# Attention with soft MoE slots: twelve more score tiles exponentiated on VectorE, in two alternating chains

## The chip, the cores and the metric

The kernel runs on one core of one Trainium2 chip, in one launch. A core has five engines with queues of their own: TensorE (PE in the profile: matmuls into PSUM), VectorE (DVE), ScalarE (ACT: activations), GpSimd (POOL) and SyncE (SP, which here issues DMAs). Each engine takes its instructions in order and waits on semaphores for the others. The metric is the device time of the launch in microseconds (us), lower is better.

## The reference

Capped softmax attention over 8 batches of 12 heads, 448 tokens and head size 64, followed by a soft mixture of experts over the 3584 tokens with 32 slots (8 experts of 4):

```python
scores = scale * np.matmul(q, k.transpose(0, 1, 3, 2))      # scale = 1/8
scores = cap * np.tanh(scores / cap)                        # cap = 30
attn = np.exp(scores - scores.max(-1, keepdims=True))
attn = attn / (attn.sum(-1, keepdims=True) + 1e-09)
x = np.matmul(attn, v)              # then (batch * seq, heads * head_dim): (3584, 768)
logits = x @ phi                    # (3584, 32)
d = softmax(logits, axis=0)         # over tokens: what goes into a slot
slot_input = d.T @ x                # 8 experts x 4 slots x 768
slot_out = relu(slot_input @ w1) @ w2
out = softmax(logits, axis=1) @ slot_out
```

## The kernel before

**Tiles and chunks.** Two heads are stacked on the 128 partitions. A *pair* has seven *score tiles*, each of 128 partitions (64 keys of each of two heads) by 448 queries; 48 pairs give 336 tiles. Six tiles make a *chunk* (the array `exs[j]`, five of them in rotation), and the loop at line 655 runs over 56 chunks. Seven chunks are one batch, so the order of the work repeats with a period of seven.

**What happens to a chunk.** TensorE makes its scores in two halves of three tiles (`qk_chunk`, line 316) into two PSUM buffers. ScalarE takes each half with one tanh of 128x1344 (`tanh_chunk`, line 325) into `exs[j]` as float16. The exponential is then made in place. ScalarE does it with one instruction for the chunk (`exp_chunk`, `exp_part`, line 329), but only for the tiles from `taken(j)` on. The first `taken(j)` tiles (none, one or two) are made on VectorE by `poly_exp`: a chain of eight instructions on 16-bit data, lines 369 to 377. Step 0 scales and shifts the float16 value into a fixed-point exponent `y`, step 1 masks out its fraction into `xf`, steps 2 to 5 evaluate a cubic of it in `xp`, step 6 adds that to `y`, and step 7 turns it into the bits of a bfloat16. Five of the steps are TENSOR_SCALAR (0, 1, 2, 4, 7), three are TENSOR_TENSOR (3, 5, 6). Each step needs the one before it. There is one `xf` and one `xp`, two tiles wide, so a chain has to be past step 6 before the next one writes them.

**After the chunk.** When the last tile of a pair lies in chunk j, TensorE multiplies the pair's exponentials with V in the iteration of chunk j + 2 (`pv_first`, `pv_tail`, `pv_rest`, line 395), and VectorE takes the reciprocal of the sums (`norm`, line 402) and multiplies (line 405). Beside that VectorE copies transposed q and k (line 278) and x (line 457) out of PSUM, and small sums (lines 500, 508, 518, 543). GpSimd casts V (line 286) and issues the DMAs of q, k and the weights (lines 117, 121, 186).

**The order is written out.** The scheduling is manual: an engine's queue is what the program issues, in that order. One iteration has the slots 0, m, e, a, b, r, c, d between its fixed steps, and `at(j, slot, f, ...)` puts a job into a slot. A slot's jobs marked "<" come first, the unmarked ones then, the ones marked ">" last. Slot "r" lies between the reciprocal and the multiplication of `norm` where the iteration has a pv. The tables `SHARE` (by j mod 7) and `EDGE` (for single chunks) say for each chunk how many tiles VectorE takes and in which chunk and slot each of the eight steps is issued:

```python
SHARE = {0: (2, ((0, "<b"), (0, ">d"), (1, ">a"), (1, ">a"), (1, ">b"), (1, ">d"), (1, ">d"), (2, ">a"))),
...
for j, (tiles, places) in shared.items():
    for n, (dj, slot) in enumerate(places):
        at(j + dj, slot, poly_exp, j, tiles, n)
```

In these tables one chain is mostly finished, up to its last steps, before the next begins. Chunks with j mod 7 in {0, 2, 4, 5} give two tiles to VectorE, 6 gives one, 1 and 3 give none: nine of the 42 tiles of a period, 67 tiles in the whole run, in 39 chunks (28 with two tiles, 11 with one).

After the loop comes a tail with the last pairs, the logits and the slots (to about 260 us), the two expert layers, and the output.

Of the kernel before, what the change touches and what calls it, by code (L numbers as in the profile page):

```python
# [12 lines left out]
U16 = mybir.dt.uint16  # L13
F16 = mybir.dt.float16
# [4 lines left out]
P = 128  # L19
# [3 lines left out]
S = 448  # L23
# [14 lines left out]
def kernel(  # L38
# [27 lines left out]
    NCH = NTILE // CH  # L66
# [66 lines left out]

    att = ExitStack()
    ld = att.enter_context(tc.tile_pool(name="ld", bufs=1))
    NP = 2
    homes = {}
    for nm in ("qk0", "ex1", "wk", "ldv", "ex2", "ex3", "vb0", "qk1", "ex4", "ex0", "vb1"):
        homes[nm] = att.enter_context(tc.tile_pool(name=nm, bufs=1))
# [1 line left out]
    vb = [homes["vb0"], homes["vb1"]]  # L141
    qk = [homes["qk0"], homes["qk1"]]
    ldv, wk = homes["ldv"], homes["wk"]
    xf = wk.tile([P, NP * S], U16, name="xf")
    xp = wk.tile([P, NP * S], F16, name="xp")
    xs = att.enter_context(tc.tile_pool(name="xs", bufs=4))
    attp = ExitStack()
    psS = attp.enter_context(tc.tile_pool(name="psS", bufs=2, space=PSUM))
    psV = attp.enter_context(tc.tile_pool(name="psV", bufs=1, space=PSUM))
# [181 lines left out]
    def exp_chunk(j):  # L331
# [1 line left out]

    SHARE = {0: (2, ((0, "<b"), (0, ">d"), (1, ">a"), (1, ">a"), (1, ">b"), (1, ">d"), (1, ">d"), (2, ">a"))),
             2: (2, ((0, ">b"), (0, "<c"), (1, ">a"), (1, "<b"), (1, "<b"), (2, "e"), (2, ">a"), (2, "<b"))),
             4: (2, ((0, ">a"), (0, ">b"), (0, "<c"), (0, ">d"), (0, ">d"), (1, ">a"), (1, "<b"), (1, ">c"))),
             5: (2, ((0, "<d"), (0, "<d"), (1, ">a"), (1, ">a"), (1, "<c"), (1, "<d"), (1, "<d"), (2, "e"))),
             6: (1, ((0, "e"), (0, ">d"), (0, ">d"), (1, ">a"), (1, ">a"), (1, ">c"), (1, "<d"), (2, "<b")))}  # L340
    EDGE = {3: (1, ((0, ">b"), (0, ">b"), (0, "<c"), (0, ">c"), (0, ">d"), (1, ">a"), (1, ">a"), (1, "<b"))),
            4: (2, ((0, "<b"), (0, ">c"), (0, ">d"), (1, "e"), (1, "<b"), (1, "<b"), (1, ">c"), (2, "r"))),
            48: (1, ((0, "e"), (0, ">d"), (0, ">d"), (1, ">a"), (1, ">a"), (1, "<c"), (1, "<d"), (2, "<b"))),
            49: (2, ((0, "<b"), (0, ">d"), (0, ">d"), (1, ">a"), (1, ">b"), (1, ">d"), (1, ">d"), (2, ">a"))),
            51: (2, ((0, "e"), (0, ">a"), (0, ">a"), (0, "<d"), (0, ">d"), (1, "e"), (1, ">b"), (1, ">c"))),
            52: (1, ((0, "<b"), (0, ">b"), (0, "<c"), (0, "<d"), (1, "e"), (1, "e"), (1, "<b"), (1, ">b"))),
            53: (1, ((0, "e"), (0, ">b"), (0, "<c"), (0, ">c"), (0, ">d"), (1, "<b"), (1, ">b"), (1, ">d"))),
            54: (1, ((0, "<d"), (0, "<d"), (0, "<d"), (1, "e"), (1, "<a"), (1, "<a"), (1, ">a"), (1, ">a")))}
    shared = {j: SHARE[j % 7] for j in range(3, NCH - 2)
              if j % 7 in SHARE and j + SHARE[j % 7][1][-1][0] < NCH - 1}  # L350
    shared.update(EDGE)

    octaves = cap * math.log2(math.e)
    base = math.ceil(octaves) + 1
    if base + octaves > 127:
        shared = {}

    def taken(j):
        return shared[j][0] if j in shared else 0
# [4 lines left out]
    def poly_exp(j, tiles, n):  # L364
        n1 = tiles * S
        t = exs[j][:, 0:tiles, :].rearrange("p u s -> p (u s)")
        y, f, p = t.bitcast(U16), xf[:, 0:n1], xp[:, 0:n1]
        steps = (
            lambda: dve.tensor_scalar(y, t.bitcast(F16), octaves * STEP, base * STEP + c0,  # L369
                                      ALU.mult, ALU.add),  # L370
            lambda: dve.tensor_scalar(f, y, STEP - 1, None, ALU.bitwise_and),  # L371
            lambda: dve.tensor_scalar(p, f, c3, c2, ALU.mult, ALU.add),  # L372
            lambda: dve.tensor_tensor(p, p, f, op=ALU.mult),  # L373
            lambda: dve.tensor_scalar(p, p, c1, None, ALU.add),  # L374
            lambda: dve.tensor_tensor(p, p, f, op=ALU.mult),  # L375
            lambda: dve.tensor_tensor(y, y, p, op=ALU.add),  # L376
            lambda: dve.tensor_scalar(y, y, 128.0 / STEP, 128.0 * (127 - base),
                                      ALU.mult, ALU.add))
        steps[n]()
# [173 lines left out]
    def at(j, slot, f, *a):  # L553
        if j < 0:
            j, slot = 0, "b"
        aux.setdefault((j, slot), []).append((f, a))
# [21 lines left out]
    for b in range(B):  # L578
        j, p = b * PER, 6 * b

        def when(nm):
            return j + WHEN[nm][0], WHEN[nm][1]
# [17 lines left out]
        if b < B - 1:  # L600
# [5 lines left out]
                at(*when("en"), e_norm, b)  # L606
            if b % 2:
                at(*when("es"), e_sums, b // 2)
    for j, (tiles, places) in shared.items():
        for n, (dj, slot) in enumerate(places):  # L610
            at(j + dj, slot, poly_exp, j, tiles, n)
    for n, job in enumerate(wjobs):
        at(1 + n * (NCH - 5) // len(wjobs), "b", *job)
    for j, slot, n in ((0, "a", 10), (0, "c", 10), (1, "b", 10), (1, "c", 8)):
# [207 lines left out]
    for n0, half in sorted(w2_spilled, key=lambda x: (x[1], x[0])):  # L822
        t = tl.tile([P, 4, HD], BF16, name=f"w2t{n0}_{half}")
# [123 lines left out]
    for n in range(B // 2 * NT):  # L947
        bb, c = divmod(n, NT)
# [15 lines left out]
        if n == NH or c == 0 or full:  # L964
            ob, n1 = wts.tile([P, 2, 2, HD], F32, name="ob", tag="w1", bufs=E), n
# [44 lines left out]
```

## Time and profile before

| | |
|---|---|
| median of 3 runs | 295.72 us (295.69 to 295.93) |
| span of the profiled execution, first to last instruction | 293.9 us |
| busy over the span: PE, DVE, ACT, POOL | 255.4, 240.4, 260.3, 138.2 us |
| VectorE, steps of `poly_exp`, 39 of each | lines 369 to 377 |
| ScalarE, tanh (line 325) | 113 instructions, 147.5 us |
| ScalarE, exponentials (line 329) | 58 instructions, 119.5 us |
| granted TensorE clock, mean over the span | 0.985 |

The span leaves out what lies around the first and the last instruction, 1.8 us against the median. In the page, the mean of an instruction is its own duration; two instructions of one engine can overlap, so a count times a mean can exceed the busy time. Where what one instruction really costs its engine is wanted, it is read from the distance between two starts. A line such as "L375 DVE TENSOR_TENSOR xp<-xp,xf" is an instruction of line 375 on VectorE that writes `xp` from `xp` and `xf`.

### The profile page before, as it was taken

How to read it: one execution, taken by the hardware profiler on the slowest of the kernel's cores; microseconds unless marked ns; L12 is line 12 of the kernel's file. 1: busy time of each engine (PE TensorE's matmuls, PEld its weight loads, DVE VectorE, ACT ScalarE, POOL GpSimd, SP SyncE). 2: the span in 40 equal slices, each digit the busy share in tenths (PEclk: the TensorE clock that was granted, in tenths of full speed). 3: DMA queues.
4: the chain of work that ended last, by engine and by line, in shares of the span. 5: the costliest groups of instructions: out<-in, count | busy, mean ns of one | idle time of the engine just before them, and what ended most of it. 6: DMA issues, size and time to landing. Idle time of an engine off the chain costs nothing.

```text
span 293.9 us, 10870 instructions
## 1 busy us (share of the span) xinstructions
PE 255.4 (87%) x4728; PEld 173.9 (59%) x4728; DVE 240.4 (82%) x554; ACT 260.3 (89%) x211; POOL 138.2 (47%) x200
## 2 busy tenths in 40 slices
PE   8898889998999899979988998899989899998620
PEld 6655556756675667556756675667566668542300
DVE  3728998999999999999999989999999976246740
ACT  4999999999999999999999999999999997237620
POOL 4593554763676367635673658365643220300000
PEclk9999999999999999999999999999999999999985
DMA  7999999999999999999999999999999567989896
GB/s 273 217 194 206 221 176 212 203 191 218 230 218 193 210 228 224 199 208 227 189 179 217 223 217 184 216 229 228 209 191 219 131 216 237 407 321 376 323 427 287
DMA packets 58561, 68.13 MB, mean 232 GB/s; under 512 B 4241, under 2 KB 54673, under 8 KB 58513
## 3 DMA queue, kind: packets, MB, share of 16 engines
q0 software_dynamic: 42448, 35.31, 77.8%
q1 hardware_dynamic: 15776, 31.89, 30.8%
q8 instruction: 37, 0.61, 0.8%
q10 hardware_dynamic: 288, 0.23, 0.2%
q14 instruction: 12, 0.09, 0.1%
HBM read 91.72 MB, written 19.27 MB: 378 GB/s over the span
## 4 chain that ended last, share of the span: by engine, by line
PE 35%; DVE 32%; ACT 21%; issue 4%; DMA 2%; POOL 2%; DVEq 0%; SPq 0%; ACTq 0%
PE pv L395 12%; ACT ex L325 11%; ACT ex L329 9%; PE sc L316 6%; DVE xq L405 4%; DVE ex L376 3%; DVE xp L375 3%; DVE xp L373 3%; DVE xf L371 2%; DVE xp L372 2%; DVE ex L369 2%; DVE kT L278 2%; DVE xp L374 2%; DVE qT L278 2%; PE so_ps L878 2%
## 5 line engine op out<-in xcount | busy, mean ns | idle before, releaser
L325 ACT ACTIVATE ex<-sc 128x1344 f16<-128x1344 f32 (+1 forms) x113 | 147.5, 1410 | 1.7 <-PE sc L316 1.6
L329 ACT ACTIVATE ex<-ex 128x1792 bf16<-128x1792 f16 (+5 forms) x58 | 119.5, 2064 | 0.1
L395 PE MATMUL pv<-vbd,ex 128*128 128x130 bf16 (+1 forms) x1610 | 94.4, 211 | 6.2 <-POOL vbd L286 2.7
L395 PEld LDWEIGHTS <-ex 128*128 128x128 bf16 (+1 forms) x1680 | 75.7, 101 | 34.1 <-PE sc L316 9.2
L316 PE MATMUL sc<-qT,kT 64*64 64x448 bf16 x672 | 70.5, 359 | 4.0 <-ACT ex L325 1.6
L286 POOL CAST vbd<-vraw 64x896 bf16<-64x896 f32 x46 | 44.1, 959 | 52.8 <-PE pv L395 37.3
L316 PEld LDWEIGHTS <-kT 64*64 64x64 bf16 x672 | 24.5, 105 | 10.0 <-issue 5.8
L405 DVE TENSOR_TENSOR xq<-pv,rec 128x448 bf16<-128x448 f32 x46 | 28.7, 624 | 1.6
L117 POOL DMA_DIRECT2D w1b<-in_moe_w_dram x32 | 24.9, 781 | 0.0
L488 POOL COPY e<-E 128x512 bf16<-128x512 bf16 x9 | 6.3, 705 | 37.4 <-PE eps L507 19.9
L376 DVE TENSOR_TENSOR ex<-ex,xp 128x896 uint16<-128x896 uint16 (+1 forms) x39 | 21.8, 559 | 1.2
L294 POOL MEMSET vbd<- 64x1 bf16 x22 | 3.0, 136 | 41.1 <-PE pv L395 41.1
L375 DVE TENSOR_TENSOR xp<-xp,xf 128x896 f16<-128x896 f16 (+1 forms) x39 | 22.0, 563 | 0.4
L373 DVE TENSOR_TENSOR xp<-xp,xf 128x896 f16<-128x896 f16 (+1 forms) x39 | 21.6, 554 | 0.7
L276 PE MATMUL qps<-ident,qb 128*64 128x128 bf16 x308 | 12.8, 221 | 8.5 <-DVE kT L278 6.6
L278 DVE COPY kT<-kps 128x896 bf16<-128x896 bf16 x23 | 14.3, 622 | 6.1 <-PE kps L276 5.7
L276 PEld LDWEIGHTS <-qb 128*64 128x64 bf16 x308 | 10.9, 109 | 13.7 <-issue 13.2
L425 PE MATMUL pv<-ones 128*128 128x57 bf16 x474 | 18.6, 188 | 0.0
L372 DVE TENSOR_SCALAR xp<-xf 128x896 f16<-128x896 uint16 (+1 forms) x39 | 17.8, 456 | 0.5
L186 POOL DMA_DIRECT2D qb<-in_q_dram x22 | 16.7, 759 | 3.0 <-DMA kraw<-in_k_dram 3.0
L371 DVE TENSOR_SCALAR xf<-ex 128x896 uint16<-128x896 uint16 (+1 forms) x39 | 17.3, 444 | 0.3
L457 DVE COPY xT<-xps 128x896 bf16<-128x896 bf16 (+1 forms) x24 | 14.4, 600 | 3.0 <-PE xps L448 2.5
(135 smaller groups left out, 365.5 us busy)
## 6 DMA issues: line engine op xcount, KB each, us to landing
w1b<-in_moe_w_dram POOLq DMA_DIRECT2D x32, 384.0 KB, 8.6
vraw<-in_v_dram SPq DMA_DIRECT2D x44, 224.0 KB, 6.1
w2d<-in_moe_w_dram POOLq DMA_DIRECT2D x21, 384.0 KB, 9.5
w2t<-w2d SPq DMA_DIRECT2D x21, 384.0 KB, 7.2
out_dram<-ob SPq DMA_DIRECT2D x7, 768.0 KB, 7.6
qb<-in_q_dram POOLq DMA_DIRECT2D x22, 224.0 KB, 7.3
kb<-in_k_dram POOLq DMA_DIRECT2D x22, 224.0 KB, 6.2
out_dram<-obh SPq DMA_DIRECT2D x23, 192.0 KB, 2.0
```

What stands on the lines that cost most here:

```text
L117: pool.dma_start(out=w1b[e][:, js, fs], in_=w1r[:, e, js, fs])
L276: pe.transpose(ps[h * HP:h * HP + HP, c, :], src[:, h, c * DH:(c + 1) * DH], ident)
L278: dve.tensor_copy(t, ps)
L286: pool.tensor_copy(vbds[Q % 2][r, :, :, c0:c0 + DH], raw[r])
L316: pe.matmul(sc[cs, u, 0:S], qkT["k", Q][r, c, cs], qkT["q", Q][r, :, cs], start=True, stop=True)
L325: act.activation(exs[j][:, half * CS + u0:half * CS + u1, :].bitcast(F16), sc[:, u0:u1, 0:S], ACT.Tanh, scale=qk_scale / cap)
L329: act.activation(exs[j][:, u0:u1, :], exs[j][:, u0:u1, :].bitcast(F16), ACT.Exp, scale=cap)
L373: lambda: dve.tensor_tensor(p, p, f, op=ALU.mult),
L375: lambda: dve.tensor_tensor(p, p, f, op=ALU.mult),
L376: lambda: dve.tensor_tensor(y, y, p, op=ALU.add),
L395: pe.matmul(out_, exs[j][r, u, q0:q0 + (HP if tail else P)], v_, start=(c == 0 and g == gs[0] < NF), stop=(c == NT - 1), skip_group_check= ...
L405: dve.tensor_tensor(xq[Q][:, h, s0:s1, :], pv[:, 0:s1 - s0, 0:DH], rec.to_broadcast([P, s1 - s0, DH]), op=ALU.mult)
```

## The change

A second, one tile wide pair of work buffers `xf[1]`, `xp[1]` is added, in a pool of its own behind the others. `SHARED` gives for each chunk the number of tiles on VectorE and which pair of buffers its chain uses; `POLY` gives for each chunk and slot the steps issued there, as (chunk of the chain, step). In `POLY` the steps of two chains, one on each pair of buffers or the end of one and the start of the next, mostly take turns. The period now has four chunks with two tiles and three with one, eleven of 42 tiles; in the run 79 tiles in 51 chunks (28 with two, 23 with one). The function's steps themselves are the same.

```diff
-    NP = 2
...
-    xf = wk.tile([P, NP * S], U16, name="xf")
-    xp = wk.tile([P, NP * S], F16, name="xp")
     xs = att.enter_context(tc.tile_pool(name="xs", bufs=4))
+    more = att.enter_context(tc.tile_pool(name="more", bufs=1))
+    room = tuple(enumerate(zip((wk, more), (2, 1))))
+    xf = [home.tile([P, n * S], U16, name=f"xf{x}") for x, (home, n) in room]
+    xp = [home.tile([P, n * S], F16, name=f"xp{x}") for x, (home, n) in room]
...
-    SHARE = {0: (2, ((0, "<b"), (0, ">d"), (1, ">a"), (1, ">a"), (1, ">b"), (1, ">d"), (1, ">d"), (2, ">a"))),
...
+    SHARED = {3: (2, 0), 4: (1, 0), 5: (1, 1), 6: (2, 0), 7: (2, 0), 8: (1, 1), 9: (2, 0), 10: (1, 1),
...
+              19: (1, 1), 20: (2, 0), 21: (2, 0), 22: (1, 1), 23: (2, 0), 24: (1, 1), 25: (2, 0), 26: (1, 1),
...
+    POLY = {(3, '>b'): ((3, 0),),
...
+            (22, '>a'): ((22, 0), (21, 3), (20, 7), (22, 1)),
+            (22, '>b'): ((21, 4), (22, 2)),
+            (22, '<c'): ((21, 5),),
+            (22, '>c'): ((21, 6),),
+            (22, '>d'): ((22, 3), (21, 7)),
+            (23, '>a'): ((23, 0), (22, 4)),
+            (23, 'r'): ((22, 5),),
+            (23, '<c'): ((23, 1),),
+            (23, '>d'): ((23, 2), (23, 3), (22, 6)),
+            (24, 'e'): ((24, 0),),
+            (24, '>a'): ((22, 7), (24, 1), (23, 4)),
+            (24, 'r'): ((24, 2),),
+            (24, '<c'): ((23, 5), (24, 3)),
+            (25, 'e'): ((23, 6), (25, 0), (23, 7)),
+            (25, '>a'): ((25, 1),),
+            (25, '>b'): ((24, 4),),
+            (25, 'r'): ((24, 5),),
+            (25, '<c'): ((25, 2),),
+            (25, '>c'): ((25, 3), (24, 6)),
...
-        y, f, p = t.bitcast(U16), xf[:, 0:n1], xp[:, 0:n1]
+        x = shared[j][1]
+        y, f, p = t.bitcast(U16), xf[x][:, 0:n1], xp[x][:, 0:n1]
...
-    for j, (tiles, places) in shared.items():
-        for n, (dj, slot) in enumerate(places):
-            at(j + dj, slot, poly_exp, j, tiles, n)
+    for (j, slot), ops in POLY.items():
+        for chunk, n in ops:
+            at(j, slot, poly_exp, chunk, shared[chunk][0], n)
```

## The prediction

> **What bounds the kernel now.** I read the page first (ScalarE, ACT, 89% busy; TensorE, PE, 87%; VectorE, DVE, 82%), then the stages. Nearly all idle time lies at the ends, so the share over the span misleads: the attention loop has to be read by itself.
>
> ```profile
> core 0: us, PE busy (x) PEld busy (x) DVE busy (x) ACT busy (x) POOL busy (x), PEclk, DMA share, GB/s
> 30.00:240.00 210.00, 192.33 (x3843) 136.05 (x3844) 198.19 (x460) 209.56 (x156) 117.86 (x167) 1.00 1.16 206
> ```
>
> In the 210 us of the loop ScalarE is busy 209.56: it is the bound. VectorE is busy 198.19, 94%. Whether the other 6% is free decides this case, because the change takes work off ScalarE and puts it on VectorE. So next the waits of VectorE in this stretch, the whole answer:
>
> ```profile
> DVE rec L402 <- PE pv L395: 2.2, 9, 0.4
> DVE xT L457 <- PE xps L448: 1.7, 3, 0.7
> DVE kT L278 <- PE kps L276: 1.4, 6, 0.6
> ```
>
> Only 5.3 us of real waiting. The rest of the 6% is small gaps, and they have a pattern, seen in VectorE's own timeline (start, duration, line):
>
> ```profile
> 130.24 0.38 DVE L375 TENSOR_TENSOR xp<-xp,xf 128x448 f16<-128x448 f16 x1
> 130.66 0.39 DVE L376 TENSOR_TENSOR ex<-ex,xp 128x448 uint16<-128x448 uint16 x1
> 130.97 0.39 DVE L371 TENSOR_SCALAR xf<-ex 128x896 uint16<-128x896 uint16 x1
> 131.39 0.59 DVE L372 TENSOR_SCALAR xp<-xf 128x896 f16<-128x896 uint16 x1
> 132.01 0.62 DVE L373 TENSOR_TENSOR xp<-xp,xf 128x896 f16<-128x896 f16 x1
> ```
>
> L376 uses what L375 has just written: it starts 0.42 us after it, 0.035 us behind its end. L371 belongs to another chain: it starts 0.31 us after L376, 0.08 us before that one ends. Over 30 to 240 us, taking starts and ends instruction by instruction: 264 starts lie on average 81 ns before the end of the one ahead, 164 lie 34 ns behind it, 31 come after a longer wait (6.3 us in all). A direct successor in the same chain thus costs about 117 ns more than a neighbour from elsewhere. That is the time the alternate placing can win.
>
> The fourth row shows the second loss: L372 took 0.59 us, where the same form takes 0.38 undisturbed. Beside it GpSimd (POOL) was issuing a DMA:
>
> ```profile
> 131.00 0.76 POOL L121 DMA_DIRECT2D w2d<-in_moe_w_dram  x1
> ```
>
> Of the 180 TENSOR_SCALAR steps of the chains in this stretch, 66 had no GpSimd instruction beside them and ran 4 ns over their undisturbed time on average; the other 114 ran 120 ns over, 14.0 us in all (86 ns for each two-tile step, 51 for each one-tile step). The TENSOR_TENSOR steps hardly moved (0.62 throughout).
>
> **The change, part by part.** One period is seven chunks. Before, it had four chunks with two tiles on VectorE and one with one; afterwards four with two and three with one. Over the run the two-tile chunks stay at 28 and the one-tile chunks go from 11 to 23: twelve more one-tile chains, and a new order.
>
> *ScalarE.* The price of a tile is read from starts, since its instructions overlap too:
>
> ```profile
> 122.76 1.91 ACT L329 ACTIVATE ex<-ex 128x1792 bf16<-128x1792 f16 x1
> 124.35 2.68 ACT L325 ACTIVATE ex<-sc 128x1344 f16<-128x1344 f32 x2
> 126.69 2.30 ACT L329 ACTIVATE ex<-ex 128x2240 bf16<-128x2240 f16 x1
> 128.65 2.78 ACT L325 ACTIVATE ex<-sc 128x1344 f16<-128x1344 f32 x2
> ```
>
> Four tiles hold ScalarE from 122.76 to 124.35, 1.59 us; five from 126.69 to 128.65, 1.96. A tile is 0.373 us (the finer stamps: 1.587 and 1.960), and twelve are 4.5 us. That is the whole possible gain.
>
> *VectorE.* The eight steps of a one-tile chain, from the groups by form over the whole run:
>
> ```profile
> L375 DVE TENSOR_TENSOR xp<-xp,xf 128x448 f16<-128x448 f16 x11 | 4.3, 391 | 0.1
> L376 DVE TENSOR_TENSOR ex<-ex,xp 128x448 uint16<-128x448 uint16 x11 | 4.3, 391 | 0.3
> L373 DVE TENSOR_TENSOR xp<-xp,xf 128x448 f16<-128x448 f16 x11 | 4.2, 381 | 0.0
> L369 DVE TENSOR_SCALAR ex<-ex 128x448 uint16<-128x448 f16 x11 | 3.9, 358 | 0.0
> L371 DVE TENSOR_SCALAR xf<-ex 128x448 uint16<-128x448 uint16 x11 | 3.7, 337 | 0.1
> L372 DVE TENSOR_SCALAR xp<-xf 128x448 f16<-128x448 uint16 x11 | 3.4, 312 | 0.3
> L374 DVE TENSOR_SCALAR xp<-xp 128x448 f16<-128x448 f16 x11 | 3.0, 275 | 0.3
> L377 DVE TENSOR_SCALAR ex<-ex 128x448 uint16<-128x448 uint16 x11 | 3.0, 270 | 0.0
> ```
>
> They sum to 2.715 us with collisions. The undisturbed times (the fastest tenth of each form, in step order 265, 266, 276, 380, 276, 383, 391, 268 ns) sum to 2.505. Twelve chains are 96 instructions:
> - Undisturbed: 12 x 2.505 = 30.1 us.
> - Every added instruction that starts 82 ns before its neighbour ends gives that back: 96 x 0.082 = 7.9.
> - Direct successors: I wrote out VectorE's queue from both tables and the loop's slots and counted pairs in which the second needs the first. There are 173 before (46 of them reciprocal then multiply) and 67 after (19, since a step is placed between them in slot "r"). 106 fewer x 0.117 = 12.4 us won.
> - So VectorE's queue grows by 30.1 - 7.9 - 12.4 = 9.8 us without collisions.
> - Collisions: 60 more TENSOR_SCALAR steps, at the one-tile mean of 51 ns, 3.0 us. Bounds: 0, if GpSimd, whose work does not change, only has so much to give; 5.2, at the two-tile mean of 86. I take 3.0, the row of the same form.
>
> [...]
>
> *Waits.* VectorE works on chunks 3 to 55 from 20.6 to 244.6 us, 224.0 us. In it, waits of over 45 ns add up to 8.0, so its queue alone needs 216.0, and afterwards 216.0 + 9.8 + 3.0 = 228.8. That is more than the 224.0 of now and than the 219.5 that ScalarE would need: VectorE becomes the bound. Which waits stay? The first (1.6 us for the first pv, chunk 3) and those of chunk 54 (0.9) stem from TensorE's order and stay. The waits in between are mostly for TensorE, itself paced by ScalarE; with VectorE late they mostly close. Those for a pv that needs a just finished chain stay: between the last step of a chain and the reciprocal behind it VectorE has 0.60 to 1.17 us of other steps in chunks 21 to 25, against 0.75 to 1.36 before. I keep 0.3 us per period, 1.8 in all. Together 4.3 us; bounds 0 and 8.0.
>
> *The rest.* Two buffers of 896 bytes in each partition, behind the others: nothing else moves. No DMA is added or moved; GpSimd, SP and TensorE keep their instructions, and where VectorE is late TensorE waits at pv, and behind it in its queue the scores of the next chunk, hence ScalarE. This is how the loss reaches the end; two score buffers and the one chunk between QK and pv let no more than a few us of lateness through unseen. TensorE was granted its full clock (1.00) at 92% busy; at 89% I cost that at nothing. If the clock did fall, the loop's TensorE work (192 us) has 18 us of room.
>
> **The sum.** 228.8 + 4.3 - 224.0 = +9.1 us. The profiled execution has a span of 293.9 us and would have 303.0. The median of the runs, 295.72, is 1.8 above the span; that lies around it and stays. 295.7 + 9.1 = 304.8 us. As a cross-check, one period: VectorE's queue without collisions goes from 26.3 to 27.9 us, ScalarE's from 29.5 to 28.8; with collisions (2.1, afterwards 2.5), 0.3 of small stretch elsewhere and 0.3 of waits VectorE needs 31.0, 1.5 more than the 29.5 of now; over six and a half periods that is 9.8.
>
> **The rivals.**
> - *ScalarE stays the bound and the gain arrives: 291.2* (295.7 - 4.5). VectorE would have to fit into 219.5. Even with no wait at all it has 225.8 without added collisions, so the 14 us of collisions would have to shrink by 6.3; to come out faster at all, by 1.8. For it: which step GpSimd meets is a matter of placing, and every step is placed anew. Against it: the load that GpSimd puts there is the same and VectorE spends more time in the steps that collide. 0.09. Landing within 0.2% (0.6 us, about what a measurement of this kernel can tell from no change): 0.03.
> - *Collisions do not grow, VectorE is the bound*: 216.0 + 9.8 + 2.5 - 224.0 = +4.3, 300.0. For it: GpSimd's work is fixed. 0.10.
> - *A convoy*: the waits do not close but grow, since a late chain makes pv late and pv the reciprocal: 8.0 kept and 0.5 us more per period, 228.8 + 8.0 + 3.2 - 224.0 = +16, 311.7. It decides when VectorE is later than TensorE at more than one reciprocal per period. Against it: the 0.94 at two of the four tight places is about the 0.9 us that a pv's last 15 matmuls took. 0.10.
> - *Alternating brings no overlap*, every added instruction at full length and no successor won: 12 x 2.715 = 32.6, so 216.0 + 32.6 + 4.3 - 224.0 = +28.9, 324.6. [...] The 264 early starts speak against it here. 0.02.
>
> **How the numbers follow.** The forecast of a VectorE bound with some more collisions has 0.66. Slower: 0.66 + 0.10 + 0.10 + 0.02 = 0.88; same 0.03; faster 0.09. The range takes in the bounds of collisions and waits: low +3.3 (the second rival, with the wait of chunk 54 gone too, rounded), 299.0; high 216.0 + 9.8 + 5.2 + 8.0 - 224.0 = +15.0, 310.5. Outside lie the faster and the equal cases, the missing overlap and part of the convoy.
>
> **What would show it.** Right: ScalarE below 97% busy in the loop, waiting for TensorE's scores, and those for VectorE at pv; VectorE with hardly a gap; direct successors down to about a third; one-tile TENSOR_SCALAR rows near or above their means of now; a chunk period of about 31 us. Wrong: ScalarE still at 99% and a period under 29.5 us, that is, VectorE's steps collide less; or waits of VectorE at the reciprocal of over 10 us in all, that is the convoy.

## The result, and the profile after

The changed kernel takes 314.4 us (median; 313.3 to 317.8) against 295.8 for the kernel before: a ratio of 1.064, 95% interval 1.057 to 1.070. It is slower by 18.5 us. Forecast were 9.1 us more, and at most 14.8: the direction was right, the size was not. The profiled execution has a span of 311.5 us.

The loop of the changed kernel, engine by engine (the window is longer because the loop is):

```profile
core 0: us, PE busy (x) PEld busy (x) DVE busy (x) ACT busy (x) POOL busy (x), PEclk, DMA share, GB/s
30.00:255.00 225.00, 193.40 (x3832) 133.96 (x3824) 219.64 (x557) 207.89 (x156) 119.71 (x165) 1.00 1.11 193
```

ScalarE, busy for 99.8% of the loop before, is at 92% (207.89 of 225). VectorE is at 97.6%; of the other 5.4 us 3.1 are waits and 2.2 the short gaps between neighbours. The waits say who holds whom, first ScalarE's, then VectorE's (the longest of the copies of x, 0.9, ends at 29.9 us, just ahead of the window), then the two of TensorE that are for VectorE's multiplication:

```profile
ACT ex L326 <- PE sc L317: 11.1, 18, 0.9
ACT E L718 <- PE lps L702: 5.8, 6, 1.2
```

```profile
DVE xT L693 <- PE xps L684: 2.4, 6, 0.9
DVE rec L638 <- PE pv L631: 0.9, 2, 0.7
DVE qT L279 <- PE qps L277: 0.5, 2, 0.3
DVE kT L279 <- PE kps L277: 0.2, 1, 0.2
```

```profile
PE pv L631 <- DVE xq L641: 12.9, 19, 1.1
PE junk L874 <- DVE xq L641: 6.7, 7, 1.0
```

(`junk` is a filler matmul whose result nobody uses; it takes the same PSUM buffer as a pv.) ScalarE, which had next to no waits, now waits 16.9 us for TensorE; TensorE waits 19.6 us for the multiplication, where in the whole run before its pv waited 1.1 us for it and the filler 1.6; VectorE waits 4.0 in all. VectorE is the bound, as forecast. But its queue is longer than the sum said, and one group shows where. VectorE's groups by form in this window, the two TENSOR_TENSOR steps of the cubic, one tile wide:

```profile
L611 DVE TENSOR_TENSOR xp<-xp,xf 128x448 f16<-128x448 f16 x22 | 16.2, 737 | 0.1
...
L609 DVE TENSOR_TENSOR xp<-xp,xf 128x448 f16<-128x448 f16 x22 | 10.4, 474 | 0.1
```

These two are the same operation on the same tiles, steps 5 and 3 of a chain. Before, they took 391 and 381 ns. Step 5 now takes 737 on average. Its place is what differs: the new table puts many of the fifth steps into slot "r", between the reciprocal and the multiplication. The timelines of VectorE and of GpSimd at one such place:

```profile
122.54 0.26 DVE L610 TENSOR_SCALAR xp<-xp 128x448 f16<-128x448 f16 x1
122.81 0.20 DVE L638 RECIPROCAL rec<-pv 128x7 f32<-128x7 f32 x1
122.93 1.05 DVE L611 TENSOR_TENSOR xp<-xp,xf 128x448 f16<-128x448 f16 x1
123.90 0.61 DVE L641 TENSOR_TENSOR xq<-pv,rec 128x448 bf16<-128x448 f32 x1
```

```profile
122.81 0.92 POOL L287 CAST vbd<-vraw 64x896 bf16<-64x896 f32 x1 [1.24 <-PE pv L631]
```

GpSimd's cast of V is released by the end of a pair's pv, because only then may the old V be overwritten. The reciprocal is released by the same event. Here they start together (122.81 both), and the cast takes 0.92 us. The step in slot "r" starts 0.12 us into it and runs 1.05 us instead of 0.38, to 0.25 us behind the end of the cast; the multiplication comes that much later. In the kernel before the same cast stood beside the reciprocal and the multiplication, which reads PSUM and was not held:

```profile
133.07 0.20 DVE L402 RECIPROCAL rec<-pv 128x7 f32<-128x7 f32 x1
133.31 0.62 DVE L405 TENSOR_TENSOR xq<-pv,rec 128x448 bf16<-128x448 f32 x1
133.85 0.61 DVE L457 COPY xT<-xps 128x896 bf16<-128x896 bf16 x1
```

```profile
133.22 0.95 POOL L286 CAST vbd<-vraw 64x896 bf16<-64x896 f32 x1
```

Here the 0.95 us of the cast lie beside 0.62 us of multiplication, and then beside a copy out of PSUM: neither is longer than elsewhere (0.62 and 0.61 us, and 0.62 is the mean of each in the loop). Counted over the whole run, 27 steps stand in slot "r" and overran their undisturbed times by 15.0 us. Of the 27, 25 lie beside a cast; the other two (at 23.2 and 156.3 us) overran by nothing. All other chain steps together overran by 9.1, less than the 15.7 of all steps before.

Beside the cast, the step with both inputs in SBUF took 1.05 us instead of 0.38, and the multiplication, one of whose inputs lies in PSUM, 0.62, its mean.

### The profile page after: what moved, and what is told of

It is laid out like the page before. It is cut to its first block, busy times and chain, and to the rows that moved or that the text cites. A ratio compares the mean times of both kernels' runs of the same rounds, so it can differ in the third digit from the quotient of the medians.

```text
span 311.5 us, 10979 instructions
## 1 busy us (share of the span) xinstructions
PE 258.0 (83%) x4728; PEld 173.7 (56%) x4728; DVE 262.3 (84%) x650; ACT 258.8 (83%) x211; POOL 140.2 (45%) x200
## 4 chain that ended last, share of the span: by engine, by line
DVE 65%; PE 20%; ACT 5%; issue 3%; DMA 2%; POOL 1%; DVEq 0%; ACTq 0%; SPq 0%
DVE xp L611 9%; DVE xq L641 8%; DVE ex L612 6%; DVE xp L609 6%; DVE ex L613 5%; PE pv L631 5%; DVE xf L607 4%; DVE xp L610 4%; DVE xp L608 4%; DVE ex L605 4%; DVE xT L693 4%; DVE qT L279 4%; DVE kT L279 3%; DVE rec L638 2%; ACT ex L326 2%
## 5 line engine op out<-in xcount | busy, mean ns | idle before, releaser
L326 ACT ACTIVATE ex<-sc 128x1344 f16<-128x1344 f32 (+1 forms) x113 | 142.5, 1292 | 12.6 <-PE sc L317 12.4
L631 PE MATMUL pv<-vbd,ex 128*128 128x130 bf16 (+1 forms) x1610 | 97.4, 213 | 23.2 <-DVE xq L641 13.7
L330 ACT ACTIVATE ex<-ex 128x1792 bf16<-128x1792 f16 (+5 forms) x58 | 108.2, 1870 | 0.1
L287 POOL CAST vbd<-vraw 64x896 bf16<-64x896 f32 x46 | 45.4, 988 | 56.1 <-PE pv L631 41.9
L611 DVE TENSOR_TENSOR xp<-xp,xf 128x896 f16<-128x896 f16 (+1 forms) x51 | 34.8, 682 | 0.5
L609 DVE TENSOR_TENSOR xp<-xp,xf 128x896 f16<-128x896 f16 (+1 forms) x51 | 28.0, 548 | 0.3
L612 DVE TENSOR_TENSOR ex<-ex,xp 128x896 uint16<-128x896 uint16 (+1 forms) x51 | 27.1, 531 | 0.1
L613 DVE TENSOR_SCALAR ex<-ex 128x896 uint16<-128x896 uint16 (+1 forms) x51 | 22.7, 446 | 0.1
L608 DVE TENSOR_SCALAR xp<-xf 128x896 f16<-128x896 uint16 (+1 forms) x51 | 20.3, 397 | 0.2
L607 DVE TENSOR_SCALAR xf<-ex 128x896 uint16<-128x896 uint16 (+1 forms) x51 | 18.5, 362 | 0.3
L661 PE MATMUL pv<-ones 128*128 128x57 bf16 x474 | 18.6, 188 | 0.0
L610 DVE TENSOR_SCALAR xp<-xp 128x896 f16<-128x896 f16 (+1 forms) x51 | 17.7, 347 | 0.2
## 6 DMA issues: line engine op xcount, KB each, us to landing
vraw<-in_v_dram SPq DMA_DIRECT2D x44, 224.0 KB, 5.6
qb<-in_q_dram POOLq DMA_DIRECT2D x22, 224.0 KB, 6.7
kb<-in_k_dram POOLq DMA_DIRECT2D x22, 224.0 KB, 5.6
```

The lines of the kernel that those rows point to most:

```text
L287: pool.tensor_copy(vbds[Q % 2][r, :, :, c0:c0 + DH], raw[r])
L326: act.activation(exs[j][:, half * CS + u0:half * CS + u1, :].bitcast(F16), sc[:, u0:u1, 0:S], ACT.Tanh, scale=qk_scale / cap)
L330: act.activation(exs[j][:, u0:u1, :], exs[j][:, u0:u1, :].bitcast(F16), ACT.Exp, scale=cap)
L631: pe.matmul(out_, exs[j][r, u, q0:q0 + (HP if tail else P)], v_, start=(c == 0 and g == gs[0] < NF), stop=(c == NT - 1), skip_group_check= ...
```

## The experiments

In what follows, "overrun" is the time of the chain steps above their undisturbed times, summed from VectorE's first chain step to the last multiplication of the loop.

**Slot r emptied.** The 27 steps go right behind the multiplication:

```diff
-            at(j, slot, poly_exp, chunk, shared[chunk][0], n)
+            at(j, "<c" if slot == "r" else slot, poly_exp, chunk, shared[chunk][0], n)
```

> The changed kernel, but every step that stood in slot r (between the reciprocal and the multiplication of a pair, 27 of them) is issued right behind the multiplication, first in slot c. Theory 1 (the steps in slot r run into GpSimd's cast of V, which starts when a pair's pv ends, and are held until it is done: 15.0 of the 24.1 us by which the chain steps overran): the cast (0.93 us) now runs beside the reciprocal and the multiplication (0.78 us together), so each step loses at most some 0.15 us: 15.0 - 4 gained, 27 x 0.117 = 3.2 lost since reciprocal and multiplication are direct neighbours again: about 8 us faster than the changed kernel, 306 (303 to 309). Theory 2 (collisions depend on how many steps there are, wherever they stand, and VectorE's longer queue is the cause): the step behind meets the same GpSimd instruction, and only the 3.2 us are lost: 315 to 318. Theory 3 (late chains make TensorE late and TensorE the reciprocal): within 2 us of the changed kernel, 312 to 316.

Measured: 300.2 us, ratio 1.015 (1.013 to 1.018) to the kernel before. That is 14 us faster than the change, more than any theory gave. The group of step 5, by form over 30 to 240 us:

```profile
L611 DVE TENSOR_TENSOR xp<-xp,xf 128x448 f16<-128x448 f16 x22 | 8.7, 395 | 0.1
```

It is back at 395 ns. The overrun fell from 24.1 to 11.9 us, VectorE's waits from 7.9 to 5.6. Theories 2 and 3 fall. The remaining 4.3 us over the kernel before are the part that the prediction had reasoned about: VectorE is still the bound.

**The same in the kernel before.** Four steps a period are moved from just ahead of the reciprocal into slot r:

```diff
-    SHARE = {0: (2, ((0, "<b"), (0, ">d"), (1, ">a"), (1, ">a"), (1, ">b"), ...
+    SHARE = {0: (2, ((0, "r"), (0, ">d"), (1, ">a"), (1, ">a"), (1, "r"), ...
-             2: (2, ((0, ">b"), ...
+             2: (2, ((0, "r"), ...
-             4: (2, ((0, ">a"), (0, ">b"), ...
+             4: (2, ((0, ">a"), (0, "r"), ...
```

> The kernel before, with four steps of each period moved into slot r, from just ahead of the reciprocal to between reciprocal and multiplication (chunks with j mod 7 in 0, 1, 2, 4; about 25 in the run). Same tiles, same buffers, same number of instructions. Theory 1: each moved step meets the cast and is held some 0.5 to 0.65 us, 12 to 16 us on VectorE, of which the 6 us of waits in the loop hide a part: 301 to 307. Theory 2: no step more, so no collision more, 25 x 0.117 = 2.9 us off VectorE's queue, and ScalarE remains the bound: 295 to 296.5.

Measured: 315.0 us, ratio 1.066 (1.062 to 1.070). With the tiles, buffers and instructions of the kernel before, this edit alone costs 19 us, as much as the whole change. One of the places, here with a TENSOR_SCALAR step:

```profile
126.05 0.21 DVE L402 RECIPROCAL rec<-pv 128x7 f32<-128x7 f32 x1 [0.23 <-PE pv L395]
126.17 1.05 DVE L371 TENSOR_SCALAR xf<-ex 128x896 uint16<-128x896 uint16 x1
127.15 0.61 DVE L405 TENSOR_TENSOR xq<-pv,rec 128x448 bf16<-128x448 f32 x1
```

What follows is from the profiled execution, the slowest of the five (319.1 us; VectorE's first chain step starts 2.9 us later in it than before). The 24 steps in slot r overran by 17.1 us. That is more than expected for each (0.71), and the waits did not hide any of it: they rose from 8.0 to 15.6. VectorE's waits over 30 to 255 us:

```profile
DVE rec L402 <- PE pv L395: 9.8, 31, 1.9
```

The late multiplication frees the PSUM buffer of pv late, so the next pv starts late (TensorE's pv waits 18.5 us for the multiplication, 1.1 before), and the next reciprocal waits for it. Here the convoy does exist.

**Without the casts.** The changed kernel and the kernel just described, with the casts left out from the third quad on (a quad, `Q`, is two pairs):

```diff
-        pool.tensor_copy(vbds[Q % 2][r, :, :, c0:c0 + DH], raw[r])
+        if Q < 2:
+            pool.tensor_copy(vbds[Q % 2][r, :, :, c0:c0 + DH], raw[r])
```

> The changed kernel without GpSimd's casts of V from the third quad of heads on (44 of 48 casts are left out, so V of these quads is missing from the result); all DMAs and all work of VectorE, ScalarE and TensorE stay. Theory 1: the chain steps lose the 19.4 us of overrun beside GpSimd's casts and copies but for some 3 us of the copies of e: 14 to 16 us faster than the changed kernel, 298 to 301, with the steps in slot r at their undisturbed times. If the issuing of DMAs on GpSimd were the main cause (4.7 us of overrun beside it): 311 to 315. Theory 3 (waits): no change, 312 to 316.

> e2_before_r (315.0) without GpSimd's casts of V from the third quad of heads on (V of these quads is missing from the result). Theory 1 (steps in slot r cost time only because of the cast beside them): the moved steps run at 0.38 and 0.27 us and the whole 19 us are gone, 293.5 to 296. If it were the late multiplication as such (TensorE waiting for the pv's buffer): 305 or more.

Measured: 295.3 us (ratio 0.998, 0.994 to 1.001) and 296.9 us (ratio 1.001, 0.997 to 1.005). The steps in slot r now overran by nothing (-0.8 and -0.9 us, that is, they ran at their undisturbed times), and 19 and 18 us are gone. The first ends 2.7 us below its range, the second 0.9 above. The casts are the cause, with slot r unchanged in both. The edit takes one thing more away: TensorE no longer waits for a cast before a pv (3.3 us in the changed kernel, 1.0 in the other), so a part of the 19 us may not be the held steps; how large it is was not shown. The DMA issues of GpSimd, the other candidate, cost the chain steps 6.5 us of overrun in the first, no less than with the casts (4.7).

**The tiles of before in the new order.** Twelve chains go back to ScalarE:

```diff
+    SHARED = {j: s for j, s in SHARED.items() if not (7 < j < 48 and j % 7 in (1, 3))}
+    POLY = {at_: kept for at_, ops in POLY.items() if (kept := tuple(x for x in ops if x[0] in SHARED))}
```

> The changed kernel with the 12 one-tile chains of chunks 8 to 45 with j mod 7 in 1 and 3 left to ScalarE again (67 tiles on VectorE as before), all other steps in the new order with both pairs of buffers. Nearly all steps in slot r belonged to these chains, so they go too. Theories 1 and 2: ScalarE is the bound again and does what it did before; VectorE's queue is shorter than before by its fewer direct successors (about 6 us) and has slack: 294.5 to 297, ScalarE over 98% busy in the loop. Theory 3 (the new order by itself makes chains late): 300 or more.

Measured: 298.0 us, ratio 1.008 (1.005 to 1.012), outside both expectations. In the loop it did what was expected: its chunks start at the same distances as before, 29.6 us a period, and ScalarE is busy without a break. The loss is at the end. VectorE and TensorE there:

```profile
239.63 0.20 DVE L640 RECIPROCAL rec<-pv 128x7 f32<-128x7 f32 x1 [0.80 <-PE pv L633]
239.75 1.34 DVE L614 TENSOR_TENSOR ex<-ex,xp 128x896 uint16<-128x896 uint16 x1
241.01 0.61 DVE L643 TENSOR_TENSOR xq<-pv,rec 128x448 bf16<-128x448 f32 x1
```

```profile
241.68 0.34 PE L876 MATMUL junk<-ones 128*128 128x384 bf16 x1 [1.52 <-DVE xq L643]
```

```profile
240.00:244.00 4.00, 2.39 (x29) 1.56 (x28) 3.83 (x10) 4.00 (x4) 0.62 (x1) 0.83 0.82 242
244.00:248.00 4.00, 4.00 (x66) 3.59 (x65) 2.02 (x7) 2.38 (x3) 0.00 (x0) 0.75 0.77 279
```

In the last fence (busy times of the engines by stages, as above) the column after GpSimd's is the granted clock of TensorE. One step was left in slot r of chunk 54. It took 1.34 us instead of 0.62, TensorE waited 1.52 us for the multiplication, and was then granted half its clock from 242.6 to 246.0 us (0.83 and 0.75 in the two stages). I first put this down to the new table of the last chunks (theory E) and tried it in two ways, by giving chunks 48 to 54 the table of before, in the kernel with slot r emptied and in the one with the 67 tiles:

> Slot r emptied as in e1_no_r, and the chains of chunks 48 to 54 as the kernel before had them (one tile less, at chunk 53). In e4_67_tiles the loop ran chunk by chunk as before, yet VectorE ended 1.7 us later and the span was 1.9 longer. Theory E (the new table of the last chunks finishes its chains too late for the last pairs): 1.5 to 2 us faster than e1_no_r, 298.0 to 299.0. Rival (the lateness of e4_67_tiles is the loop's, or noise): 299.8 to 300.6.

> e4_67_tiles with the few steps left in slot r moved out and the end of the kernel before: 66 tiles in the new order, ScalarE the bound. Theory E: the 1.9 us of e4_67_tiles come back, 295.4 to 296.5, as the kernel before. Rival (the new order costs the end something through the loop): 297.5 to 298.5. Either way it shows what the alternating order is worth by itself where ScalarE is the bound: nothing.

Measured: 300.6 us (ratio 1.015, 1.012 to 1.019) and 295.5 us (ratio 0.999, 0.996 to 1.001). The first shows no effect of the table; the second does gain, but it had lost its steps in slot r too. So the next run has the table of the change, with those steps alone moved:

> e4_67_tiles with its three last steps in slot r issued behind the multiplication; the table of the last chunks stays. In e4_67_tiles one of them, in chunk 54, stood beside a cast and took 1.34 us instead of 0.62; TensorE sat idle for 1.5 us until the multiplication and was then granted half its clock for 3.4 us. Theory 1 (that one step makes the late end, through TensorE's clock): no half clock at the end of the loop, 295 to 296.5, as e12_m13_end. Theory E (the table of the last chunks): 297.5 to 298.5, as e4_67_tiles.

Measured: 295.5 us, ratio 0.999 (0.996 to 1.001), and no half clock in the loop. Theory E falls. The two profiles run alike, chunk by chunk (their starts on ScalarE are 0.2 to 0.3 us apart up to the last chunk), and part only behind the step in chunk 54, though all three steps were moved. It was that one step in slot r, 0.7 us late and worth about 2 us in the end (2.0 in the spans, 2.5 in the medians). Through TensorE's clock it was about 1.7, an estimate from 3.4 us at half speed. These two runs also give the worth of the alternating order by itself: none that can be measured, since ScalarE bounds and VectorE's saving turns into waits (18.6 us in all, 8.0 before).

**Fewer tiles.** Slot r empty, the end of the kernel before, and of the twelve chains only those of j mod 7 = 1 left to ScalarE, or only those of j mod 7 = 3 (72 tiles on VectorE in either), or three of the latter (75 tiles):

```diff
+    SHARED = {j: s for j, s in SHARED.items() if not (7 < j < 48 and j % 7 in (3,))}     # 72 tiles, (1,) in the other
+    SHARED = {j: s for j, s in SHARED.items() if j not in (10, 24, 38)}                  # 75 tiles
```

> As e8_end, with only the six one-tile chains of chunks with j mod 7 = 1 left to ScalarE: 72 tiles on VectorE. VectorE's queue of e1_no_r, 228.9 us with 5.6 of waits, loses 6 x 1.86 and some 1 us of overrun: 216 to 217, below ScalarE's 224.0 - 5 x 0.373 = 222.1. ScalarE is the bound: 293.5 to 294.5, faster than before by 1.5 to 2. Rival (VectorE's load within the period is uneven, so single chunks still hold TensorE up): 295.5 to 297.5.

> As e9_m1_end, but the chains of j mod 7 = 3 are the ones left out: the same sums, 293.5 to 294.5 if they alone decide. Its steps stand in other places (chunks 10 to 12 instead of 8 to 10 of a period), so a difference of more than 0.7 us between the two shows that the place in the period counts and not the sum alone.

> e10_m3_end with the chains of chunks 17, 31 and 45 back: 75 tiles. ScalarE saves 3 x 0.373 = 1.1 us more than in e10_m3_end; VectorE gets 5.6 us more and had 10.0 us of waits there. By the sums ScalarE stays the bound: 0.5 to 1.1 us faster than e10_m3_end, ratio to before 0.990 to 0.993. Rival (VectorE fills unevenly, and the periods with three one-tile chains run at e1_no_r's 30.5 us): 1 to 3 us slower than e10_m3_end, ratio 0.998 to 1.004.

Measured: 297.6 us (ratio 1.006, 1.004 to 1.009), 294.1 us (ratio 0.994, 0.991 to 0.997), and 296.2 us (ratio 1.001, 0.999 to 1.004). The second is faster than both kernels, by 0.6% against before; its loop:

```profile
30.00:230.00 200.00, 186.40 (x3698) 129.52 (x3696) 190.79 (x492) 199.96 (x151) 119.25 (x163) 1.00 1.19 210
```

ScalarE is the bound again with 199.96 of 200, with five tiles fewer in the run than before. With three chains more the gain is gone: VectorE's waits are down from 10.0 to 8.1 us, and ScalarE no longer runs without a break (197.67 of 200). The first has as many tiles as the second. In the profiles, counted from the first chunk, its last chunk starts 4.7 us later than the second's, and 2.4 of these come in at one place. Its timeline there (VectorE, GpSimd, TensorE):

```profile
127.81 0.95 POOL L287 CAST vbd<-vraw 64x896 bf16<-64x896 f32 x1 [2.93 <-PE pv L646]
127.89 1.35 DVE L626 TENSOR_TENSOR xp<-xp,xf 128x896 f16<-128x896 f16 x1
...
129.16 0.19 DVE L653 RECIPROCAL rec<-pv 128x7 f32<-128x7 f32 x1
...
130.16 0.94 PE L646 MATMUL pv<-vbd,ex 128*128 128x130 bf16 x12 [1.62 <-DVE xq L656]
```

No step stands in slot r here. VectorE had simply come late: pv was done and had released the cast while VectorE still had a two-tile step ahead of the reciprocal. That step met the cast (1.35 us instead of 0.62), the reciprocal came 1.3 us after the end of pv, TensorE sat idle for 1.62 us and got half its clock from 130.8 to 134.2 (0.60 granted over 130 to 134 us). The period around it took 32.2 us instead of 29.4. The same step was held in the same way (1.35 us, TensorE idle for 1.62) in the kernel with slot r emptied, where no half clock followed, and its period took 31.3 us. The other 2.3 us come in bit by bit at other chunks and were not traced to a cause, and only one run of this kernel was profiled (298.9 us, 1.3 above the median): why the two kernels differ is shown in part.

## Why the prediction was right in direction and too small

By its own terms, for VectorE from the first chain step to the last multiplication of the loop (224.0 us before, 242.0 after):

| term | predicted | measured |
|---|---|---|
| queue without collisions (96 steps more, less overlap and fewer direct successors) | +9.8 | +9.7 (+28.8 work, -19.1 overlap and gaps) |
| collisions with GpSimd | +3.0 (0 to 5.2) | +8.4 (15.7 to 24.1) |
| waits | -3.7 (to 4.3) | -0.1 (8.0 to 7.9) |
| sum | +9.1 | +18.0 |

- **The bound passes from ScalarE to VectorE: right**, by the busy times and the waits above. A period takes 32.1 to 33.0 us instead of the 31 forecast. The price of a tile on ScalarE, 0.373 us, fits the better run with 72 tiles (five tiles, 1.9 us by the price, 1.8 measured), but here the saving does not come to count.
- **The queue: right to 0.1 us, in part by luck.** The added work was 1.3 us less than the 30.1 of the sum and the savings 1.2 less than its 20.3, and the two cancel. Independent neighbours overlap, as read from the starts (454 of 30 to 240 us lie ahead of the end of the neighbour, 264 before); the rival without overlap (324.6) is out. But the saving on the pair of reciprocal and multiplication, 27 x 0.117 = 3.2 us of the 12.4 in that step of the sum, was booked as a gain of slot r, without asking what runs beside that slot.
- **Collisions: this step failed.** I priced each added TENSOR_SCALAR step with the mean overrun of its form and gave TENSOR_TENSOR nothing, since "0.62 throughout" was what the trace showed. Both were averages over places in which the cast of V lay beside the multiplication. The collision depends on the place: 27 steps in slot r account for 15.0 us, and outside it the overrun fell by 6.6 us although 60 TENSOR_SCALAR steps were added. By kind of step, counted from the same two traces, the overrun of the TENSOR_TENSOR steps went from 0.9 to 11.6 us, 8.5 of it in slot r, and that of the TENSOR_SCALAR steps from 14.5 to 11.9: the whole growth lies in the term that was put at nothing. That TENSOR_TENSOR reads two SBUF inputs and could be held as well (1.05 us beside the cast) was neither a term nor a rival. With slot r empty the kernel takes 300.2 us, what the rival "collisions do not grow" gave (300.0); so close by luck, since the overrun is then 3.8 us below that of before, the waits are 5.6 instead of the 2.5 kept, and the 3.2 us are lost.
- **The range.** Its upper bound was added up to +15.0, which is 310.7 us and not 310.5; the measured 314.4 lies above either.
- **Waits: also too small.** Of the 7.9 us left, 3.2 lie ahead of chunk 7 and 1.6 before copies of x in the middle, near what I kept; but 3.1 lie from 230 us to the end of the loop, where I had kept 0.9.
- **"At 89% busy I cost the clock at nothing": wrong.** In the profiled run of the changed kernel TensorE had half its clock (0.50 granted) from 258.5 to 261.9 us, behind a step in slot r of chunk 54; 3.4 us at half speed are about 1.7 us (an estimate), and between the two runs with 67 tiles the same step and the event behind it were worth about 2.
- **The convoy rival** gave the nearest time, 311.7, and was the wrong mechanism for this kernel: VectorE's waits at the reciprocal are 0.9 us in the window. It is the right one for the kernel before with steps in slot r (9.8 us).

## What to carry to other kernels

When a step is moved into a gap of one engine, ask what the same event releases on the others: here the end of pv released both the reciprocal and GpSimd's cast, and the gap behind the reciprocal, free by VectorE's own queue, was the worst place of the period for a step that reads SBUF (15.0 us of overrun for 27 steps, 9.1 for all other chain steps). A mean overrun of a group is an average over places and can't price a new place; read what stands beside the slot in the other engines' timelines. And a queue with little slack loses its shields: a late VectorE meets the cast with steps that had been clear of it, as in the place shown (1.35 us instead of 0.62). The best share of those tried was 72 tiles, with 10.0 us of waits left; 75 tiles left 8.1 and lost the gain, and so did 72 tiles in other chunks, so the places count beside the number.

## What the runs showed of the hardware that was not expected

- A TENSOR_TENSOR step with both inputs in SBUF that started during GpSimd's cast of SBUF data was held until the cast was done (1.05, 1.34 and 1.35 us instead of 0.38 and 0.62), and a TENSOR_SCALAR step likewise (1.05 instead of 0.38). These steps ended 0.25 us (those of 0.38) or 0.48 us (those of 0.62) behind the end of the cast, so all but about 0.14 us of their own time came after it. The multiplication, with one input in PSUM, was not held (0.62 beside the cast).
- It was the later one that was held. Where a TENSOR_TENSOR step of the changed kernel started 0.13 us ahead of the cast, the step kept its 0.62 us and the cast took 1.30 instead of 0.95, in six places of the run. One of them:

```profile
128.26 0.62 DVE L612 TENSOR_TENSOR ex<-ex,xp 128x896 uint16<-128x896 uint16 x1
```

```profile
128.38 1.30 POOL L287 CAST vbd<-vraw 64x896 bf16<-64x896 f32 x1
```

- Where TensorE had waited 1.2 to 1.6 us in one piece, 3.4 us at half its clock (0.50 granted from 258.5 to 261.9 us in the changed kernel) followed in four of the profiled runs: in chunk 54 of the changed kernel and of the one with 67 tiles (1.52 each), in the kernel before with steps in slot r (1.16), and in one with 72 tiles (1.62). Of the 16 waits of 1.15 us or more in the loops of all profiles, these four were followed by it; a wait of 1.62 us in the kernel with slot r emptied and one of 1.60 in the kernel before with steps in slot r passed without it. So the length of the wait alone does not decide. What does was not shown.
